# Storing each batch's gates as four rows of 448 bytes, turned on the chip first, in place of 448 elements of 4 bytes

## The chip, the cores and the metric

The kernel runs on one core of one Trainium2 chip. The time is device microseconds (us) of one launch. One launch computes an attention layer, a mixture of experts with one expert per token, and a second dense layer with a normalisation.

## The reference

Four batches of 448 tokens (1792 in all) go through three parts:

```python
scores = scale * (q_n @ k_n^T)            # q, k normalised by their root mean square; 12 heads of 64
x = softmax(scores) @ v                   # (4, 12, 448, 64) -> 1792 x 768

logits = x @ w_gate                       # 1792 x 8
expert_idx = argmax(logits, axis=1)
gate_w = softmax(logits)[token, expert_idx]
out[token] = gate_w * (relu(x @ w1[e]) @ w2[e])      # e: the token's own expert, 768 -> 1024 -> 768

h = out @ w_in; solu = h * softmax(h)     # 768 -> 1024
y = layernorm(solu) * g_ln @ w_out        # 1024 -> 768
```

The change touches the way in which `gate_w`, one number for each token, gets to a table in device memory.

## The kernel before, in words

Attention and routing come first, to about 318 us of the profile. They are not written in program order: each piece of work is a task with an engine, an estimated duration, a priority, what it depends on, and the ring buffers that it takes or uses. The class `Work` (L31) walks through all tasks, at each step takes from those that can start earliest the one of the lowest priority number, and issues its instructions. The order on each engine is therefore the outcome of the whole list: a task that is added, or that asks for a buffer, can move every task that is placed after it. Once issued, each engine executes its instructions strictly in that order, and an instruction that waits holds up all behind it.

Attention works on pairs of heads, six for each batch. For each pair GpSimd (POOL) scales the inputs, TensorE (PE) transposes them (L435), ScalarE (ACT) and VectorE (DVE) split them in a high and a low part (L458, L461), SyncE (SP) starts DMAs that move halves between partitions (L468, tiles `KS`, `QQ`, `K2`, `Q2`), PE multiplies (L497), DVE takes maxima (L508), which are transposed (L520) and copied to `mr` on ACT or DVE (L526, L528), ACT takes exponentials, high and low parts are made (L555, L558), and PE multiplies with the values (L587 to L589, tile `av`). The finished 448 x 128 block `x` goes to the device-memory table `xd` (L721), is transposed (L728) and multiplied with the router's weights (L739).

PSUM buffers for most of PE's short results form one ring `r` of four, named r_99 to r_102 in the instruction lists: a task that takes one waits until all readers of its last holder are done.

After the sixth pair of a batch, `Routing.route` (L761) works out for its 448 tokens, laid out as 112 partitions x 4 columns: the expert (L782 to L840), each token's rank among its expert's tokens (L790 to L797 on PE, L842, L843), four one-hot compares (L809, tile `ohr`), the list of tokens of each expert (L815, 12 short matmuls; L824, L826 or L828), and the gate: exponentials (L855), their sum (L856, L857), its reciprocal `gt` (L832). The gate is stored to the device-memory table `gd`, of one column, with a DMA on SP (L859). `gd` is read much later, by small gathers (L1569).

After the last batch, the lists `gx` are copied to a second table (L984 to L990). GpSimd then gathers the rows of `xd` that belong to each expert (L1129, `gx<-xd,gx`); PE transposes the first expert's rows (L1175) and the experts start (L1154 onwards). Expert weights come by DMA on SP (L1104, `wr`).

Of the kernel before, what the change touches and what calls it, by code (L numbers as in the profile page):

```python
# [7 lines left out]
F32 = mybir.dt.float32  # L8
# [8 lines left out]
CP = 112  # L17
NC = 4
D = 64
S = 448  # L20
# [10 lines left out]
class Work:  # L31
# [11 lines left out]
               DVE=dict(PE=0.2, ACT=0.14, DVE=0.13, Pool=0.16, SP=0.1), Pool=dict(PE=0.2, ACT=0.2, DVE=0.2, Pool=0.0, SP=0.1),  # L43
# [15 lines left out]
    def add(self, eng, dur, fn, deps=(), prio=0.0, take=(), use=(), lat=0.0, dma=0.0):  # L59

        t = len(self.tasks)
        e = eng if isinstance(eng, dict) else {eng: dur}
        self.tasks.append((e, fn, [d for d in deps if d is not None], prio, take, lat, dma))
        for u in list(take) + list(use):
            self.users.setdefault(u, []).append(t)
        return t
# [106 lines left out]
class Attention:  # L173
# [8 lines left out]

    RINGS = dict(
        kq=2, v=2, sq=2, u=2, gsc=3, vj=1, va=3, X=3, op=6, K2=4, mx=2, mr=2, st=2, pf=5, pp=2, r=4, av=2, den=2,
    )

    def __init__(self, nc, ctx, tc, kq, v, ident, groups, work):
# [16 lines left out]
        ps = P("ps", 1, space=PSUM)  # L204
        R = self.RINGS
        for r in ("st", "r", "av"):
# [10 lines left out]
    def start(self, g_qk):  # L217
        nc = self.nc
        R = self.RINGS

# [433 lines left out]
class Routing:  # L654
# [44 lines left out]
        self.gx = C("gx", [128, RT * E_], I32)  # L699
        self.sum = self.acc_d = self.li_d = None  # L700

    RINGS = dict(x=3, xT=2, lg=2, rt=1, gt=2)

    def start(self, w, w_gate, more):

# [55 lines left out]
    def route(self, w, b, prio, M=None, order=None):  # L761

        nc, W = self.nc, self.pool
        V = nc.vector
# [5 lines left out]
        t = {}  # L770
        own = ("rt", b)
        add = lambda eng, dur, fn, deps, take=(), use=(), lat=0.0: w.add(
            eng, dur, fn, deps, prio, take, [own, *use], lat
        )
# [59 lines left out]
        lg, rk, li, gt = ("lg", b), ("r", f"rk{b}"), ("r", f"li{b}"), ("gt", b)  # L834
        d = w.add("DVE", 0.1, room, [self.sum, *self.init_d], prio, take=[own], use=[lg])
        d_s = d = add("DVE", 0.1, lambda e: V.tensor_tensor(t["ls"], self.lg, bc(t["mx"]), op=ALU.subtract), [d], use=[lg])

        d = add("DVE", 0.1, lambda e: V.scalar_tensor_tensor(t["oh"], t["ls"], 0.0, self.desc, op0=ALU.is_ge, op1=ALU.mult), [d])
        d = add("DVE", 0.1, lambda e: V.tensor_reduce(t["cm"], t["oh"], axis=AX.X, op=ALU.max), [d])
        d_o = add("DVE", 0.1, lambda e: V.tensor_tensor(t["o16"], self.desc, bc(t["cm"]), op=ALU.is_equal), [d])  # L840
        d = d_r = add("PE", 0.2, rank, [d_o, self.acc_d], take=[rk])
        d = add("DVE", 0.1, lambda e: V.tensor_tensor(t["rkt"], t["z"].rearrange("p (c e) -> p c e", e=E_), t["o16"], op=ALU.mult), [d], use=[rk])  # L842
        d = add("DVE", 0.1, lambda e: V.tensor_reduce(self.rk[:, bs], t["rkt"], axis=AX.X, op=ALU.add), [d])  # L843
        d_t = add("DVE", 0.1, lambda e: V.tensor_tensor(tk, t["o16"], bc(self.tid[:, bs]), op=ALU.mult), [d_o])
        if M is not None:
# [4 lines left out]
        d = add("PE", 0.28, lists, dd + [d_t], take=[li])  # L850
        d_l = self.li_d = add("DVE", 0.1, total, [d, self.li_d, order], use=[li])
        d = add("DVE", 0.1, lambda e: V.tensor_reduce(t["oc"], t["o16"].rearrange("p c e -> p e c"), axis=AX.X, op=ALU.add), [d_o])
        self.acc_d = add("DVE", 0.1, lambda e: V.tensor_tensor(self.acc, self.acc, t["oc"], op=ALU.add), [d, d_r])

        d = add("ACT", 0.2, lambda e: nc.scalar.activation(t["ls"], t["ls"], AF.Exp), [d_s, d_o])  # L855
        d = add("DVE", 0.1, lambda e: V.tensor_reduce(t["sm"], t["ls"], axis=AX.X, op=ALU.add), [d])  # L856
        d = add("DVE", 0.1, lambda e: V.tensor_scalar(t["sm"], t["sm"], 1e-9, None, op0=ALU.add), [d])  # L857
        d = add("DVE", 0.1, gate, [d], take=[gt])
        add("SP", 0.5, lambda e: nc.sync.dma_start(  # L859
            self.gd[b * S : (b + 1) * S, :].rearrange("(c p) e -> p c e", c=NC), t["gt"]  # L860
        ), [d], use=[gt], lat=1.5)

    def zeros(self):

# [508 lines left out]
def body(tc, kq, v, g_qk, w_gate, wmoe, w_in, w_out, g_ln, out):  # L1373
    nc = tc.nc
    ctx = ExitStack()
    with ctx, tc.manual_schedule():
# [12 lines left out]
        rpool = P(att_ctx, "route", 1)  # L1389
        work = Work({**Attention.RINGS, **Routing.RINGS})  # L1390
        att = Attention(nc, att_ctx, tc, kq, v, ident, GROUPS, work)
# [462 lines left out]
```

## Time and profile before

| | us |
|---|---|
| three runs | 896.51, 899.03, 904.44 |
| median | 899.03 |
| profiled execution, its own time | 896.94 |
| its span, first to last instruction | 895.2 |

Busy time in the span is 811.1 us on PE (91%), 641.4 on DVE (72%), 497.8 on ACT (56%) and 395.1 on POOL (44%). The 16 DMA engines are busy 40.8% of the span for the queue of SP and 4.0% for that of GpSimd. The profile's own time is 2.1 us below the median of the three runs. Attention and routing with the first gathers take the span to 336 us, the experts to about 650 us, the second layer the rest.

### The profile page before, as it was taken

The page shows a single profiled execution, that of the slowest core. Times are in us where ns is not written, and L with a number is a line of the kernel's source. Part 1 is how long each engine was busy: PE and PEld are TensorE (multiplying, and loading weights), DVE is VectorE, ACT ScalarE, POOL GpSimd, SP SyncE. Part 2 cuts the span into 40 slices and gives each one's busy share as a digit, 9 for nine tenths or more (in the row PEclk, how much of TensorE's full clock was granted, in tenths as well). Part 3 has the DMA queues.
Part 4 walks back from the last instruction along what each step waited for, and adds up shares of the span by engine and source line. Part 5 has one row for each costly group of instructions (what it writes and reads, how often), then busy time and mean ns, then how long its engine had stood idle before and what let it go on. Part 6 is the DMA issues. An engine that isn't in the chain of part 4 may idle for free.

```text
span 895.2 us, 18893 instructions
## 1 busy us (share of the span) xinstructions
PE 811.1 (91%) x6811; PEld 740.8 (83%) x6811; DVE 641.4 (72%) x1484; ACT 497.8 (56%) x958; POOL 395.1 (44%) x420
## 2 busy tenths in 40 slices
PE   2788998987898959989999999899899999999994
PEld 2577887776787849979999999789779989998994
DVE  7988998897898937998667778788575434444541
ACT  7787988886885805644455556667532323332221
POOL 4777898787784624543674125545110000000000
PEclk9999999999997979999999999999999999999998
DMA  7476575574743355757666777767000000000001
GB/s 207 125 200 171 134 197 145 146 197 83 198 111 83 117 118 164 222 187 244 209 220 202 260 229 250 243 211 245 2 1 36 19 36 19 18 18 36 19 18 38
DMA packets 63871, 120.29 MB, mean 134 GB/s; under 512 B 12159, under 2 KB 35290, under 8 KB 63774
## 3 DMA queue, kind: packets, MB, share of 16 engines
q1 hardware_dynamic: 60478, 107.69, 40.8%
q0 software_dynamic: 3296, 11.35, 4.0%
q8 instruction: 56, 0.92, 0.4%
q14 instruction: 41, 0.34, 0.1%
HBM read 86.08 MB, written 11.03 MB: 108 GB/s over the span
## 4 chain that ended last, share of the span: by engine, by line
PE 36%; issue 26%; DVE 17%; DMA 13%; ACT 4%; POOL 2%; SPq 1%; POOLq 0%; ACTq 0%; DVEq 0%
DMA out_dram<-ot,tok 5%; PE st L497 4%; DMA QQ<-QQ 3%; PE h L1157 3%; DVE mx L508 2%; PE h L1158 2%; PE y L1157 2%; PE h L1159 2%; PE y L1158 2%; PE y L1159 2%; PE r L497 2%; PE h L1154 2%; DMA gx<-xd,gx 2%; PE y L1154 2%; DMA rkq<-in_kq_dram 2%
## 5 line engine op out<-in xcount | busy, mean ns | idle before, releaser
L558 POOL TENSOR_TENSOR pl<-pf,ph 128x448 f16<-128x448 f32 x153 | 166.1, 1105 | 47.7 <-ACT ph L555 16.8
L1359 POOL DMA_INDIRECT out_dram<-ot,tok x14 | 13.8, 987 | 214.3 <-ACT ot L1358 208.8
L508 DVE TENSOR_REDUCE mx<-r 128x1 f32<-128x448 f32 x168 | 99.4, 611 | 12.3 <-PE r L497 11.9
L1114 POOL TENSOR_TENSOR wl<-wr,wh 128x768 fp32r<-128x768 f32 x34 | 64.5, 1899 | 93.6 <-ACT wh L1109 93.1
L1109 ACT CAST wh<-wr 128x768 fp32r<-128x768 f32 x128 | 104.7, 831 | 1.6 <-DMA wr<-in_wmoe_dram 1.6
L1114 DVE TENSOR_TENSOR wl<-wr,wh 128x768 fp32r<-128x768 f32 x94 | 97.5, 1037 | 10.5 <-ACT wh L1109 9.0
L551 ACT ACTIVATE pf<-st 128x448 f32<-128x448 f32 x168 | 86.7, 544 | 22.0 <-PE st L497 19.5
L497 PE MATMUL r<-KS,QQ 128*128 128x448 f32 x192 | 69.0, 428 | 21.0 <-DMA QQ<-QQ 12.1
L555 ACT CAST ph<-pf 128x448 f16<-128x448 f32 x153 | 82.5, 569 | 0.3
L587 PEld LDWEIGHTS <-ph 128*128 128x128 f16 x768 | 71.0, 97 | 12.0 <-issue 10.9
L587 PE MATMUL av<-va,ph 128*128 128x65 f16 x768 | 80.1, 194 | 0.0
L588 PE MATMUL av<-va,ph 128*128 128x64 f16 x768 | 79.7, 195 | 0.0
L589 PE MATMUL av<-va,pl 128*128 128x65 f16 x768 | 79.3, 193 | 0.0
L497 PE MATMUL st<-QQ,KS 128*128 128x448 f32 x192 | 74.4, 408 | 2.7 <-ACT pf L551 2.6
L1320 DVE TENSOR_TENSOR cl<-ct,ch 128x512 fp32r<-128x512 f32 x28 | 18.1, 686 | 80.3 <-ACT ch L1319 80.2
L589 PEld LDWEIGHTS <-pl 128*128 128x128 f16 x768 | 71.6, 99 | 0.0
L588 PEld LDWEIGHTS <-ph 128*128 128x128 f16 x768 | 71.4, 97 | 0.1
L497 PE MATMUL st<-Q,K 128*128 128x448 f32 x192 | 68.7, 378 | 0.5 <-DMA K<-KS 0.5
L1154 PE MATMUL y<-hh,wh 128*128 128x384 f32 (+1 forms) x192 | 61.0, 354 | 7.7 <-DVE hh L1203 7.4
L1154 PE MATMUL h<-xx,wh 128*128 128x384 f32 (+1 forms) x192 | 63.0, 364 | 0.4 <-DVE xx L1184 0.4
L497 PEld LDWEIGHTS r<-KS,QQ 128*128 128x128 f32 x192 | 35.5, 199 | 31.1 <-DVE mx L508 5.9
L1157 PE MATMUL h<-xx,wh 128*128 128x280 f32 (+1 forms) x192 | 57.4, 299 | 0.7 <-DVE hh L1203 0.7
(282 smaller groups left out, 2525.9 us busy)
## 6 DMA issues: line engine op xcount, KB each, us to landing
wr<-in_wmoe_dram SPq DMA_DIRECT2D x128, 384.0 KB
rkq<-in_kq_dram SPq DMA_DIRECT2D x24, 448.0 KB
di<-in_w_in_dram SPq DMA_DIRECT2D x16, 384.0 KB
rv<-in_v_dram SPq DMA_DIRECT2D x24, 256.0 KB
do<-in_w_out_dram SPq DMA_DIRECT2D x16, 384.0 KB
K<-KS SPq DMA_DIRECT2D x48, 112.0 KB
KS<-Q SPq DMA_DIRECT2D x48, 112.0 KB
QQ<-QQ SPq DMA_DIRECT2D x48, 112.0 KB
```

The source lines that it names most:

```text
L497: nc.tensor.matmul(ps[:, :S], H[w][x + "x"][:, columns(w, s)], H[w][y], start=(k == 0), stop=(k == len(n) - 1))
L508: V.tensor_reduce(C["mx"][:, s : s + 1], C["sm", s][:, :S], axis=AX.X, op=ALU.max, negate=True)
L551: nc.scalar.activation(C["pf", s], C["st", s][:, :S], AF.Exp)
L555: (eng[e].copy if e == "ACT" else eng[e].tensor_copy)(ph[s][:, :S], C["pf", s])
L558: eng[e].tensor_tensor(pl[s][:, :S], C["pf", s], ph[s][:, :S], op=ALU.subtract)
L587: nc.tensor.matmul(o, hp, vs[:, 0:65], start=(s == ss[0]), stop=False)
L588: nc.tensor.matmul(o[:, 0:64], hp, vs[:, 65:129], start=False, stop=False)
L589: nc.tensor.matmul(o, lp, vs[:, 0:65], start=False, stop=(s == ss[-1]))
L1109: self.nc.scalar.copy(wh, raw)
L1114: (eng or self.nc.vector).tensor_tensor(wl, raw, f32(wh), op=ALU.subtract)
L1154: mm(ps[:, : 2 * n], wh, xx[:, : 2 * n], start=start, stop=False)
L1157: mm(ps[:, :n], wh, xh, start=start, stop=False)
```

## The change

The gates `gt` (112 partitions x 4) are transposed on PE into a buffer of the ring `r`, which gives four rows of 112, copied by DVE to a new tile `gq` (4 partitions x 112, two buffers), and stored from there. The table `gd` gets the same bytes at the same places. The four stores had 448 pieces of 4 bytes each; now they have four pieces of 448 bytes each.

```diff
-    RINGS = dict(x=3, xT=2, lg=2, rt=1, gt=2)
+    RINGS = dict(x=3, xT=2, lg=2, rt=1, gt=2, gq=2)
...
         d = add("DVE", 0.1, gate, [d], take=[gt])
+        gr, gq = ("r", f"gr{b}"), ("gq", b)
+
+
+        def rows(e):
+            t["gr"] = w.buf(*gr)
+            nc.tensor.transpose(t["gr"][:NC, :CP], t["gt"][:, :, 0], self.ident[:CP, :CP])
+
+        def copy_rows(e):
+            t["gq"] = W.tile([NC, CP], F32, tag="gq", name=f"gq{b}", bufs=2)
+            V.tensor_copy(t["gq"], t["gr"][:NC, :CP])
+
+        d = add("PE", 0.11, rows, [d], take=[gr], use=[gt])
+        d = add("DVE", 0.12, copy_rows, [d], take=[gq], use=[gr])
         add("SP", 0.5, lambda e: nc.sync.dma_start(
-            self.gd[b * S : (b + 1) * S, :].rearrange("(c p) e -> p c e", c=NC), t["gt"]
-        ), [d], use=[gt], lat=1.5)
+            self.gd[b * S : (b + 1) * S, :].rearrange("(c p) e -> c (p e)", c=NC), t["gq"]
+        ), [d], use=[gq], lat=1.5)
```

Eight instructions are new: four transposes on PE (L864) and four copies on DVE (L868). The store is L872 afterwards, and lines behind it have moved by 13. Up to the routing of the first batch the order is the same as before; from there on every engine's order differs. By count, six copies of maxima to `mr` change from ACT to DVE (18 and 6 before, 12 and 12 after) and so does one making of a high part (153 on ACT before, 152 after).

On SP, around the store of the second batch (`KS`, `K`, `QQ`, `Q` are the moves between partitions; K is `K2` and Q is `Q2`), before:

```order
L468 DMA KS_130<-Q_142 64x448
L859 DMA gd<-gt_3651 112x4x1
L721 DMA xd<-x_1_3483 112x4x128
L468 DMA K_145<-KS_129 64x448
L468 DMA QQ_136<-QQ_136 64x448
L468 DMA KS_125<-QQ_131 64x448
L468 DMA K_146<-KS_130 64x448
L531 DMA Q_139<-mr_115 1x4x128
L531 DMA Q_140<-mr_115 1x4x128
L468 DMA KS_125<-Q_137 64x448
```

and after:

```order
L721 DMA xd<-x_1_3482 112x4x128
L468 DMA QQ_135<-QQ_135 64x448
L872 DMA gd<-gq_3677 4x112
L468 DMA KS_130<-QQ_136 64x448
L468 DMA K_145<-KS_129 64x448
L468 DMA KS_130<-Q_142 64x448
L468 DMA KS_125<-QQ_131 64x448
```

The store of the block `xd` stood right behind that of the gates and now stands two places ahead of it.

On DVE, in the routing of the third batch, before (`ohr` are the one-hot compares, `sm` the sum of exponentials, r_99 to r_102 the ring `r`):

```order
L809 TENSOR_SCALAR ohr_3_4815<-cols,rk 112x384
L857 TENSOR_SCALAR sm_4588<-sm_4588 112x4
L461 SCALAR_TENSOR_TENSOR Q_142<-r_102,G,QQ_136 128x448
L603 TENSOR_SCALAR den_4848<-av_103,ve_3930 112x4
L832 RECIPROCAL gt_4851<-sm_4588 112x4
L508 TENSOR_REDUCE mx_113<-r_99 128x1
```

and after:

```order
L809 TENSOR_SCALAR ohr_3_4833<-cols,rk 112x384
L857 TENSOR_SCALAR sm_4606<-sm_4606 112x4
L508 TENSOR_REDUCE mx_113<-r_100 128x1
L603 TENSOR_SCALAR den_4865<-av_103,ve_3911 112x4
L832 RECIPROCAL gt_4867<-sm_4606 112x4
L508 TENSOR_REDUCE mx_113<-r_102 128x1
L614 RECIPROCAL den_4865<-den_4865 112x4
L826 TENSOR_TENSOR lists<-lists,r_100 128x24
L508 TENSOR_REDUCE mx_113<-r_99 128x1
L608 TENSOR_TENSOR x_1_4894<-av_103,den_4865 112x4x64
L868 COPY gq_4901<-r_102 4x112
```

and on PE at the same place, after:

```order
L815 LDWEIGHTS ohr_3_4833
L815 MATMUL r_100<-tk,ohr_3_4833 128x8
L497 MATMUL st_97<-QQ_131,KS_125 128x448
L497 MATMUL st_97<-Q_137,K_145 128x448
L864 MATMUL r_102<-ident,gt_4867 4x112
L497 MATMUL st_98<-QQ_131,KS_125 128x448
L497 MATMUL st_98<-Q_137,K_145 128x448
```

Behind the compares DVE had a split that frees r_102; now it has two maxima there, which free r_100 for the list matmuls and r_102 for the new transpose, and the gates in between.

On DVE, in the last batch, after:

```order
L832 RECIPROCAL gt_5644<-sm_5618 112x4
L809 TENSOR_SCALAR ohr_0_5646<-cols,rk 112x384
L809 TENSOR_SCALAR ohr_1_5649<-cols,rk 112x384
L809 TENSOR_SCALAR ohr_2_5651<-cols,rk 112x384
L809 TENSOR_SCALAR ohr_3_5653<-cols,rk 112x384
L868 COPY gq_5655<-r_100 4x112
L828 SCALAR_TENSOR_TENSOR gx<-r_102,lists 128x24
```

The copy is the only new row there; it stands between the last compare and the lists.

## Rows read from the trace of the kernel before

**Rows 1.** Windows by stage: busy us of each engine, granted clock, DMA share, GB/s.

```profile
200.00:300.00 100.00, 89.89 (x1131) 79.22 (x1131) 84.34 (x215) 75.68 (x155) 68.64 (x66) 0.93 0.47 112
...
318.00:336.00 18.00, 8.00 (x54) 6.88 (x53) 4.29 (x25) 0.49 (x3) 4.91 (x5) 0.64 0.51 103
```

**Rows 2.** Instructions on the table gd: duration min/median/max in ns, first and last start.

```profile
L859 SPq DMA_DIRECT2D gd<-gt x4: 330/517/537, 135.8 to 321.6; - x4
```

**Rows 3.** DMA queue of SP, 281 to 281.25 us: packets, MB, share of 16 engines.

```profile
q1 hardware_dynamic: 345, 0.00, 70.5%
```

**Rows 4.** Timeline of SP, second batch's store: start us, us, what.

```profile
210.30 0.54 SPq L859 DMA_DIRECT2D gd<-gt  x1
210.93 0.51 SPq L721 DMA_DIRECT2D xd<-x  x1
...
218.85 0.54 SPq L468 DMA_DIRECT2D KS<-Q  x1
```

**Rows 5.** Waits of SP from 208 to 220 us: total us, times, longest.

```profile
SPq L468 <- DMA gd<-gt: 2.3, 1, 2.3
```

**Rows 6.** Windows of 1 us behind the second batch's store, columns as in rows 1.

```profile
212.00:213.00 1.00, 1.00 (x11) 0.94 (x9) 1.00 (x3) 0.96 (x3) 1.00 (x2) 1.00 0.79 215
...
215.00:216.00 1.00, 1.00 (x15) 0.65 (x11) 0.88 (x3) 1.00 (x3) 1.00 (x2) 1.00 1.67 106
...
217.00:218.00 1.00, 0.00 (x0) 0.00 (x0) 0.22 (x1) 0.42 (x2) 1.00 (x2) 1.00 0.41 47
```

**Rows 7.** DMA queue of SP, 213.25 to 213.5 us, as in rows 3.

```profile
q1 hardware_dynamic: 4, 0.00, 196.9%
```

**Rows 8.** Windows of 1 us behind the first and the third batch's store.

```profile
140.00:141.00 1.00, 1.00 (x9) 0.95 (x8) 1.00 (x3) 0.97 (x3) 1.00 (x2) 1.00 0.49 115
...
287.00:288.00 1.00, 1.00 (x5) 0.87 (x4) 0.00 (x0) 0.65 (x2) 0.34 (x1) 0.50 0.51 148
```

**Rows 9.** Timeline of PE from 218.5 us, with idle time before and what ended it.

```profile
219.43 0.64 PE L497 MATMUL r<-KS,QQ 128*128 128x448 f32 x2 [3.39 <-DMA Q<-mr]
```

**Rows 10.** Window of 1 us behind that wait.

```profile
221.00:222.00 1.00, 1.00 (x6) 0.87 (x6) 0.75 (x2) 0.00 (x0) 0.00 (x0) 0.50 0.28 67
```

**Rows 11.** Timeline of POOL: the first expert's first gather.

```profile
324.08 1.19 POOL L1129 DMA_INDIRECT gx<-xd,gx  x1 [10.18 <-DVE pl_gf L984]
```

**Rows 12.** Timeline of PE from 326 us: transposes of the gathered rows.

```profile
332.77 1.51 PE L1175 MATMUL yx<-ident,gx 128*128 128x128 f32 x6 [5.82 <-DMA gx<-xd,gx]
335.22 0.90 PE L1175 MATMUL yx<-ident,gx 64*128 64x64 f32 x6 [0.94 <-DMA gx<-xd,gx]
```

**Rows 13.** DMA queue of GpSimd, 326 to 328 us, then 420 to 422 us.

```profile
q0 software_dynamic: 13, 0.08, 86.2%
...
q0 software_dynamic: 103, 0.53, 83.3%
```

**Rows 14.** Window of the experts' first us, columns as in rows 1.

```profile
335.00:340.00 5.00, 4.39 (x19) 4.21 (x20) 1.68 (x6) 1.43 (x6) 0.48 (x1) 0.50 0.15 48
```

**Rows 15.** Timelines of DVE and PE, last batch's routing.

```profile
323.00 0.18 DVE L828 SCALAR_TENSOR_TENSOR gx<-r,lists 128x24 int32<-128x24 f32 x1 [0.50 <-PE r L873]
...
321.87 1.09 PE L815 MATMUL r<-tkr,ohr 112*128 112x8 f16 x12 [1.27 <-DVE ohr L809]
```

**Rows 16.** Timelines of DVE and PE, third batch's routing, and the window behind it.

```profile
274.71 3.06 DVE L809 TENSOR_SCALAR ohr<-cols,rk 112x384 f16<-112x384 f16 x3
...
279.33 1.01 PE L728 MATMUL r<-ident,x 112*128 112x112 f32 x4 [2.53 <-DVE Q L461]
...
278.50:289.00 10.50, 9.67 (x63) 8.45 (x63) 7.39 (x20) 4.71 (x9) 3.53 (x5) 0.51 0.20 45
```

**Rows 17.** Groups by line and shape, 100 to 325 us: busy, mean ns of one.

```profile
L520 PE MATMUL r<-ident,mx 128*7 128x128 f32 x17 | 4.6, 272 | 0.0
...
L528 DVE TENSOR_SCALAR mr<-r 7x128 fp32r<-7x128 f32 x4 | 1.1, 273 | 1.2 <-PE r L520 1.2
...
L555 DVE CAST ph<-pf 128x448 f16<-128x448 f32 x11 | 5.7, 516 | 0.0
```

## The prediction, made before the result was known

> **What bounds the kernel now.** I read the windows by stage first. Up to 318 us no engine is the bound by itself: PE, DVE, ACT and POOL wait for each other in short turns, with PE and DVE the fullest (89.89 and 84.34 us of 100 from 200 to 300 us) [rows 1]. Between 318 and 336 us nearly everything stands: PE is busy 8.00 of 18 us, at a mean granted clock of 0.64 [rows 1]. There the last batch's routing, the lists and the first gather follow one another, and each us is a us of the launch. From 336 us the experts keep PE busy, so an earlier start of the experts carries to the end, and a later one too.
>
> The four stores of gates that change are small in every view: SP spends 517 ns on the issue of one [rows 2], and in the fullest quarter of a us 345 of the 4-byte packets take 70.5% of 16 engines [rows 3], which is 0.705 x 0.25 x 16 / 345 = 8 ns each, so about 0.25 us for 448 of them if 16 engines share them. By that the change would be worth nothing. So I looked at what happens behind each store.
>
> Behind the second batch's store something does. It is issued at 210.30 us, and the store of `xd` right behind it [rows 4]. The next us of packets is normal (215 GB/s at 0.79 of the engines). Then the DMA engines are full and move little: 106 GB/s at a share of 1.67, then 47 GB/s at 0.41 [rows 6], and in one quarter of a us four packets take 196.9% of 16 engines, 2.0 us each [rows 7]. SP stands 2.3 us for the landing of the gate store and goes on at 218.85 us [rows 5, 4], 8.55 us after its issue. [...] I call this the wake of the store.
>
> The last batch's store, at 321.6 us [rows 2], is followed by the stores of the table `tab` and then by the first expert's gather, issued at 324.08 us [rows 11]. From 326 to 328 us GpSimd's queue moves 13 packets with 86.2% of 16 engines: 0.862 x 2 x 16 / 13 = 2.1 us each. In a later gather it is 103 packets with 83.3%, 0.26 us each [rows 13]. The 2.1 us is the same as in the second batch. PE waits 5.82 and 0.94 us for the two gathers and begins the second at 335.22 us [rows 12].
>
> Against a common cause speak the first and the third store. Some us behind them, at 140 and 287 us, 115 and 148 GB/s move at shares of 0.49 and 0.51, as in any quiet stretch [rows 8]. What differs is the next write: behind the second store comes `xd`, behind the fourth `tab`, behind the first and third no further write to device memory for some us. My theory is that 448 writes of 4 bytes land slowly, over some 7 us, and that another write to device memory behind them, within that time, fills the engines.
>
> **The change part by part.** *The last batch's gather.* A later gather moves 0.53 MB in 2 us [rows 13]. The first two gathers are 192 rows of 3 KB, 0.59 MB, 2.2 us at that pace, and one load of weights beside them (128 x 768 numbers, 0.39 MB) another 1.5 us. The first issue ends at 325.27 us (324.08 + 1.19) [rows 11], so both could have landed at 329.0, where PE begins at 335.22: 6.2 us. The second gather is issued later than the first and the third and fourth share the engines, so I take 5.0, between 0 (the wake is not the store's) and 6.2. Next late then is the gathers' own transfer. A shorter stop could also keep PE's clock up: from 335 to 340 us it is 0.50 [rows 14], which would give 2.5 us more; I take none of it.
>
> *The second batch's wait.* The stop of 3.39 us [rows 9] and some 3 us at half clock behind it (1.6 us lost) give at most 5.0. The moves would need some time to land in any case, and the new order puts `xd` ahead of the store. I take 1.5, between 0 and 5.0.
>
> [...]
>
> *What is added.* Four transposes on PE, by the nearest row (a transpose to 7 x 128) 0.27 us each, and four copies on DVE, by the copy of 7 x 128 out of PSUM 0.27 us each [rows 17]. In the last batch both are hidden: PE idles 1.27 us ahead of the list matmuls, and the gates are ready ahead of the compares; the copy stands in the 0.50 us in which DVE waits for PE ahead of `gx` [rows 15]. Without that cover it would be 0.3 us on the path. The store itself comes some 1 us later on SP, ahead of the stores of `tab`, which wait for a later instruction of DVE. In the other three batches DVE is nearly full: 3 x 0.27 = 0.8 us, between 0 and 1.6 (PE's part too).
>
> *What is moved.* Everything behind the first batch's store (135.8 us) [rows 2] is placed anew. By count DVE gets six copies of maxima (0.27) and one cast (0.52) from ACT [rows 17]: 2.2 us more on an engine that is one of the two fullest. I take half, 1.1, between 0 and 2.2.
>
> *The new waits.* PE's transpose waits for the gates and for its buffer, and all of PE's later work is queued behind it. In the first two batches the order leaves PE enough ahead of it. In the third, the list matmuls and then the transpose wait for DVE, which makes the compares (three take 3.06 us), a maximum, the gates and a second maximum first. The old order stops PE at the same place: 2.53 us for a split behind the compares, and 9.67 us of work at a clock of 0.51 behind it [rows 16], which costs about 9.67 x 0.49 = 4.7. A stop for a stop, I take 0, between -7.2 (it is gone, with its slow clock) and +7.2 (a second one like it).
>
> Sum: -5.0 - 1.5 + 0.8 + 1.1 + 0 = -4.6 us. The profiled execution took 896.94 us, so 892.3; its own time is 2.1 below the median of 899.03, so the median of new runs may lie up to 2 us higher. I predict 892.
>
> **The rivals.** *The wake is not the store's, or stays.* The slow packets at 326 us are the first of GpSimd's queue, and two of the four stores show no wake. Then the first two terms are 0: 896.94 + 1.9 = 898.8 us.
>
> *PE waits at the new transpose.* It ends on the other side. In the third batch L864 stands two matmuls behind the lists, and needs a gate and a buffer that DVE gives four places behind its last compare. If PE empties there, and the clock falls, each such stop costs up to 7.2 us. It decides from a stop of about 2 us, since the old one was 2.53. With one stop and no gain at the gather: 898.8 + 7.2 = 906.0; with a second one in the second batch 913.
>
> *More than the sum.* PE's stop in the third batch goes (-7.2), and the experts begin at full clock (-2.5): 892.3 - 9.7 = 882.6 us. For it speaks that both stops follow from DVE's or the gather's lateness alone; against it that the new DVE order has as many rows behind its compares.
>
> **How the numbers follow.** I give the forecast 0.50, no wake 0.22, the new wait 0.12, more than the sum 0.16. A range from 883 to 903 leaves out about half of the last case and most of the third, 0.19 in all. The three runs before lie 7.9 us apart, so 1% (9.0 us, 890.0 to 908.0) is about what a measurement can tell from no change. Faster by more: the last case and 0.10 of the forecast, 0.26. Slower by more: 0.07, of the third case. The rest, 0.67, is within 1%.
>
> **What would show it.** Right: the first packets of GpSimd's queue at about 0.3 us each, PE's transposes of the second gather some 6 us behind the first gather's issue, where they are 11.1 us behind now, no stretch in attention with a share over 0.9 and under 110 GB/s, SP never standing for a gate store. Wrong: the same 2 us packets behind the new stores; a wait of PE at L864 of over 1 us, or the end of attention moved by more than 5 us, by an order that no row here prices. The last is the likeliest way to be wrong, in either direction.

## The result, and the profile after

The changed kernel takes 888.68 us (median of six runs, 882.16 to 892.86) where the kernel before took 899.18 in the runs beside it: a ratio of 0.9869 with a 95% interval of 0.9823 to 0.9915. Six more runs gave 890.52 us and 0.9849 (0.9806 to 0.9892). So it is faster by 1.3 to 1.5%. The profiled execution took 887.74 us, its span is 886.0, 9.2 us less than before.

The first gather, on POOL's and PE's timelines of the changed kernel (start us, us, engine, line, what; in brackets the idle time before and what ended it):

```profile
318.12 1.19 POOL L1142 DMA_INDIRECT gx<-xd,gx  x1 [11.06 <-DMA gd<-gq]
...
323.16 1.51 PE L1188 MATMUL yx<-ident,gx 128*128 128x128 f32 x6 [1.87 <-DMA gx<-xd,gx]
324.83 0.90 PE L1188 MATMUL yx<-ident,gx 64*128 64x64 f32 x6 [0.16 <-DMA gx<-xd,gx]
```

From the issue to the transposes of the second gather it is 6.71 us, where it was 11.14 [rows 11, 12]. The issue itself comes 5.96 us earlier, so 4.4 us were gained in the gather and 6.0 ahead of it. (The bracket names the landing of the new store as what released the gather, but the issue comes 5.18 us behind L782 of the last batch in both kernels, so this costs nothing.) Some 1.2 us of the 10.4 are given back among the experts.

GpSimd's queue from 320 to 322 us, behind the new store (packets, MB, share of 16 engines):

```profile
q0 software_dynamic: 66, 0.37, 69.4%
```

That is 0.694 x 2 x 16 / 66 = 0.34 us for a packet, where it was 2.1 [rows 13].

Windows of the changed kernel, columns as in [rows 1]: the third batch's routing, a stretch in the second batch, the experts' first us:

```profile
278.50:289.00 10.50, 10.50 (x141) 9.34 (x140) 10.00 (x25) 8.43 (x17) 6.79 (x6) 1.00 0.35 89
199.00:210.00 11.00, 10.54 (x93) 9.71 (x93) 6.99 (x23) 7.13 (x16) 5.21 (x5) 0.54 0.46 130
...
325.00:330.00 5.00, 4.61 (x21) 4.43 (x22) 1.68 (x6) 1.71 (x8) 0.88 (x1) 0.54 0.19 70
```

The stretch that ran at a clock of 0.51 behind the third batch's stop [rows 16] is at 1.00 and PE is never idle in it. There is a new slow stretch at 199 us in this execution; in that of e11, the same kernel, the same window has a clock of 0.95. The experts begin at a clock of 0.54, where it was 0.50 [rows 14].

The new instructions on PE and DVE: duration min/median/max in ns, first and last start:

```profile
L864 PE MATMUL r<-ident,gt x4: 259/260/346, 138.8 to 315.7; 112*4 112x112 f32 x4
...
L868 DVE COPY gq<-r x4: 252/252/255, 139.7 to 316.5; 4x112 f32<-4x112 f32 x4
```

### The profile page after: what moved, and what is told of

The parts are those of the page before. It is cut to its first block, busy times and chain, and to the rows that moved or that the text cites. A ratio compares the mean times of both kernels' runs of the same rounds, so it can differ in the third digit from the quotient of the medians.

```text
span 886.0 us, 18898 instructions
## 1 busy us (share of the span) xinstructions
PE 810.0 (91%) x6815; PEld 739.9 (84%) x6815; DVE 641.6 (72%) x1495; ACT 497.9 (56%) x951; POOL 397.3 (45%) x420
## 4 chain that ended last, share of the span: by engine, by line
PE 38%; issue 26%; DVE 14%; DMA 13%; ACT 4%; POOL 2%; SPq 1%; another core or an unknown queue 1%; POOLq 0%; ACTq 0%; DVEq 0%
DMA out_dram<-ot,tok 5%; PE st L497 5%; PE r L497 3%; PE h L1170 3%; DMA QQ<-QQ 2%; PE h L1171 2%; PE h L1167 2%; PE h L1172 2%; PE y L1170 2%; DMA KS<-QQ 2%; PE y L1171 2%; PE y L1172 2%; DMA rkq<-in_kq_dram 2%; DVE mx L508 2%; PE y L1167 2%
## 5 line engine op out<-in xcount | busy, mean ns | idle before, releaser
L1127 DVE TENSOR_TENSOR wl<-wr,wh 128x768 fp32r<-128x768 f32 x94 | 97.0, 1032 | 11.1 <-ACT wh L1122 9.4
L587 PEld LDWEIGHTS <-ph 128*128 128x128 f16 x768 | 71.4, 98 | 12.4 <-issue 11.1
L497 PE MATMUL r<-KS,QQ 128*128 128x448 f32 x192 | 66.0, 415 | 14.0 <-DMA QQ<-QQ 9.3
L588 PEld LDWEIGHTS <-ph 128*128 128x128 f16 x768 | 71.8, 98 | 0.2
L423 POOL TENSOR_TENSOR X<-rkq,y 128x512 f32<-128x512 f32 (+1 forms) x48 | 47.7, 1006 | 19.0 <-DVE y L347 16.0
```

What stands on the lines that cost most here:

```text
L497: nc.tensor.matmul(ps[:, :S], H[w][x + "x"][:, columns(w, s)], H[w][y], start=(k == 0), stop=(k == len(n) - 1))
L587: nc.tensor.matmul(o, hp, vs[:, 0:65], start=(s == ss[0]), stop=False)
L588: nc.tensor.matmul(o[:, 0:64], hp, vs[:, 65:129], start=False, stop=False)
L1127: (eng or self.nc.vector).tensor_tensor(wl, raw, f32(wh), op=ALU.subtract)
```

## The experiments

All kernels are listed here, because the stages tell more than the totals. The three stages are the times between the starts of the routing's first maximum (L782) of batches 1 to 4 on DVE, each from one profiled execution; "gather" is the time from the issue of the first gather to PE's second six transposes. Each ratio is to runs of the kernel before on the same chip, so compare kernels by the ratios and not by the times. In the kernel before, for example, L782 starts at 118.58, 191.65, 265.90 and 318.90 us.

| kernel | order | store | us | ratio to before, 95% | 1-2 | 2-3 | 3-4 | gather |
|---|---|---|---|---|---|---|---|---|
| before | old | 448 x 4 B | 899.18 | | 73.1 | 74.3 | 53.0 | 11.1 |
| e1 | new | 448 x 4 B | 903.53 | 1.0015 (0.9987-1.0044) | 76.1 | 70.2 | 57.0 | 11.9 |
| e4 | old | 448 x 4 B, write behind | 904.51 | 1.0024 (0.999-1.0058) | 78.0 | 74.7 | 51.7 | 11.5 |
| e6 | old | 448 x 4 B, ACT's queue | 903.35 | 1.0016 (0.9985-1.0047) | 76.0 | 79.7 | 49.0 | 12.1 |
| e2 | old | 4 x 448 B | 892.57 | 0.9915 (0.9886-0.9943) | 72.3 | 75.2 | 52.3 | 6.5 |
| e3 | old | 112 x 16 B | 888.39 | 0.9834 (0.978-0.9887) | 72.1 | 71.8 | 53.0 | 6.8 |
| e10 | old | 448 x 16 B | 894.66 | 0.9905 (0.987-0.9941) | 73.3 | 71.1 | 53.0 | 6.6 |
| e7 | old | one of 16 x 448 B | 892.64 | 0.9886 (0.9845-0.9928) | 73.7 | 72.7 | 51.8 | 6.3 |
| changed | new | 4 x 448 B | 888.68 | 0.9869 (0.9823-0.9915) | 72.6 | 71.5 | 49.5 | 6.7 |
| e11, the same | new | 4 x 448 B | 890.52 | 0.9849 (0.9806-0.9892) | 71.4 | 70.9 | 49.8 | 6.9 |
| e8 | new | one of 16 x 448 B | 885.66 | 0.9849 (0.9802-0.9897) | 72.5 | 68.7 | 49.0 | 7.8 |
| e12, as e8 | new | one of 16 x 448 B | 890.80 | 0.9846 (0.9806-0.9885) | 72.0 | 70.4 | 49.0 | 7.0 |

In e2 PE makes all twelve transposes without a stop, the first of them 4.93 us behind the issue.

**e1, the new order with the old form.**

```diff
-            self.gd[b * S : (b + 1) * S, :].rearrange("(c p) e -> c (p e)", c=NC), t["gq"]
-        ), [d], use=[gq], lat=1.5)
+            self.gd[b * S : (b + 1) * S, :].rearrange("(c p) e -> p c e", c=NC), t["gt"]
+        ), [d], use=[gq, gt], lat=1.5)
```

> The changed kernel with its order, transposes and copies, but each store again writes 448 pieces of 4 bytes from the untransposed gates, at the place where the changed kernel stores the rows. Theory of the wake (small pieces, and a write to device memory behind them): in this order no such write follows the second batch's store closely, but the table's store follows the fourth, so the second batch stays without a stop and the first gather is slow again, some 11 us from its issue to PE's transposes of the second gather (6.7 in the changed kernel): 4.4 us over the changed kernel, 893 us, ratio to before 0.993. Rival, the order alone makes the gain: as the changed kernel, 888.7 us, 0.988, gather at 6.7 us. Rival, any store of this form slows what comes behind it: stops behind two or more of the stores, 897 us or more.

It measured 903.53 us, a ratio of 1.0015 whose interval holds 1: the last rival, and not the 0.993 that I expected. The gather is slow, and SP stands behind the first and the third store, where I had seen no wake. SP's waits in the 10 us behind the third store of e1 (total us, times, longest), and the move in question on its timeline:

```profile
SPq L468 <- DMA KS<-QQ: 4.3, 1, 4.3
```

```profile
283.15 0.46 SPq L468 DMA_DIRECT2D KS<-QQ  x1
...
289.45 0.46 SPq L468 DMA_DIRECT2D QQ<-QQ  x1
```

The same place in the changed kernel, whose order is the same:

```profile
SPq L468 <- DMA KS<-QQ: 0.2, 1, 0.2
```

```profile
279.33 0.46 SPq L468 DMA_DIRECT2D KS<-QQ  x1
...
281.51 0.46 SPq L468 DMA_DIRECT2D QQ<-QQ  x1
```

`QQ<-QQ` overwrites what `KS<-QQ` reads, so it waits for the landing of that move: 2.18 us behind its issue in the changed kernel, 6.30 us in e1. The windows of e1 show nothing of it, since the engines are nearly or wholly idle meanwhile:

```profile
287.00:288.00 1.00, 1.00 (x29) 1.00 (x29) 1.00 (x4) 0.86 (x2) 0.97 (x2) 1.00 0.16 16
288.00:289.00 1.00, 1.00 (x28) 0.99 (x26) 0.86 (x1) 0.07 (x1) 1.00 (x2) 1.00 0.00 0
```

The kernel before has the same thing in its first batch, where I had looked at windows only [rows 8]. SP's waits in the 10 us behind its first store:

```profile
SPq L468 <- DMA KS<-QQ: 2.2, 1, 2.2
```

and PE behind them:

```profile
147.00 0.64 PE L497 MATMUL r<-KS,QQ 128*128 128x448 f32 x2 [2.17 <-DMA QQ<-QQ]
```

In all four kernels with 448 x 4 bytes PE has such a stop behind the first store, of 2.16 to 2.83 us; in the eight others no stop of PE for a move in stage 1-2 is over 1.5 us.

**e2, the new form in the old order.**

```diff
...
-            V.reciprocal(t["gt"], t["sm"])
+            V.reciprocal(t["gt"], t["sm"].to_broadcast([CP, NC, 28]))
...
-            self.gd[b * S : (b + 1) * S, :].rearrange("(c p) e -> p c e", c=NC), t["gt"]
+            self.gd[b * S : (b + 1) * S, :].rearrange("(c p) e -> c (p e)", c=NC),
+            t["gt"][:NC].rearrange("p c e -> p (c e)")
```

> The kernel before, with its order and without transposes, but each store writes four pieces of 448 bytes. What is left out: the rows hold the gates of four partitions, repeated, and not each token's own, so the output is scaled by wrong gates. Theory of the wake: no packets of 2 us behind any store, the gather at 6 to 7 us (4.4 gained), no wait of SP for the gate store in the second batch (1.5 to 5 gained), the stop in the third batch stays: 890 to 893 us, ratio 0.990 to 0.993. Rival, the order alone makes the gain: 899 us, ratio 1.000, with the wake or the stops as before. Rival, all of the gain is the form's: 888.7 or less, 0.988.

It measured 892.57 us, 0.9915: as the theory of the wake has it. SP waits for no landing in the 10 us behind any of the first three stores. The third batch's stop stays as it was:

```profile
281.25 0.60 PE L728 MATMUL r<-ident,x 112*128 112x112 f32 x4 [2.53 <-DVE Q L461]
```

**e3, 112 pieces of 16 bytes in the old order.**

```diff
-            self.gd[b * S : (b + 1) * S, :].rearrange("(c p) e -> p c e", c=NC), t["gt"]
+            self.gd[b * S : (b + 1) * S, :].rearrange("(p c) e -> p (c e)", c=NC), t["gt"][:, :, 0]
```

> The kernel before, with its order, but each store writes 112 pieces of 16 bytes (the four gates of a partition side by side). What is changed: the gates stand at other tokens' places in the table. If the wake counts by pieces: a quarter of its length, about 2 us behind the second and the fourth store in place of 7, the time within 1 us of the kernel with four pieces of 448 bytes. If any store of small pieces has it: as before, 899 us, packets of 2 us for some 7 us. If order makes the gain and not the store: 899 us too, but without a change of the gather.

It measured 888.39 us, 0.9834, without a late move and with a gather of 6.8 us. A quarter of the pieces, at 16 bytes, leaves nothing of the wake where I had expected a quarter of its length. That pieces of this size make it is out.

**e4, a write behind the first and third store.**

```diff
...
+            if b in (0, 2):
+                nc.sync.dma_start(
+                    self.sd[b * S : (b + 1) * S, :].rearrange("(c p) e -> p c e", c=NC),
+                    self.zero[:CP, :512].rearrange("p (c e) -> p c e", c=NC),
+                )
```

> The kernel before with one more store of 112 x 4 x 128 zeros to an unused table, right behind the gate stores of the first and the third batch, where none follows before. Theory of the wake: a second and a third wake there, full DMA engines with packets of about 2 us for some 5 us around 140 and 285 us, and late moves between partitions: 901 to 909 us, ratio 1.002 to 1.011. Rival, the wake belongs to the second batch's and the gather's own neighbours: no full engines there, only two issues of 0.5 us on SP and 1.3 us of transfers, 899 to 900 us.

It measured 904.51 us; the interval of the ratio holds 1. Behind the third store the engines are full for 1 us (a window of e4), behind the first SP takes 3.58 us over the issue of one move (its timeline):

```profile
290.00:291.00 1.00, 1.00 (x7) 1.00 (x7) 1.00 (x2) 0.55 (x1) 0.64 (x1) 0.50 1.38 133
```

```profile
144.23 3.58 SPq L468 DMA_DIRECT2D K<-KS  x1
```

So the time doesn't decide, and the trace shows the theory half right at most. A write behind isn't needed for a late landing (e1). It may lengthen it: in the first batch SP issues the `QQ<-QQ` that waits for the move 9.9 us behind the store, against 7.5 us before, but PE's stop there is 2.23 us against 2.17.

**e6, the old store on ACT's queue.**

```diff
-        add("SP", 0.5, lambda e: nc.sync.dma_start(
+        add("SP", 0.5, lambda e: nc.scalar.dma_start(
```

> The kernel before with its order and its form of store, issued from ACT's queue at the same place of the program and not from SP's. Theory that landings are held up in the order of one queue: SP no longer waits for moves behind the first three stores, about 4 of the 7.7 us that the form alone gains are seen, the gather stays slow (its cause is the write, not SP's queue): 895 to 897 us, ratio 0.995 to 0.997. Rival, the 4-byte writes hold up the engines or the memory for all queues: late moves as before, 899 us or more, ratio 1.00 to 1.005.

It measured 903.35 us, 1.0016, the rival. SP waits 2.4 us for a move in the first batch and 3.3 us for the landing of the store in the second. The order within one queue is not what holds the moves.

**e5 and e9, trials behind the work.** Each trial issues a store, a move of 64 x 448, and a small transfer that waits for the move.

```diff
...
+            if k != "m":
+                dma(dst(s), src)
+            dma(mv[64:128], a[0:64, :448])
+            dma(dv[0:1, :4], mv[64:65, :4])
```

> The kernel before, and behind all of its work twelve trials on SP's queue, with no other transfers: a store of one form (or none), a move of 64 x 448 between partitions right behind it, a small transfer that waits for the move, and a second store to the same table that waits for the first. SP's issue times give the landings. Theory (a store of many 4-byte pieces lands late, and what is queued behind it lands no sooner): the move alone 2 to 2.5 us; behind 448 pieces of 4 bytes 5 to 8 us, as the store itself; behind 4 pieces of 448, 112 of 16 or 448 of 512 bytes as alone, within 1 us. Of the dose: 112 pieces of 4 bytes a quarter of the delay, 224 a half, if pieces count. With 448 pieces of 4 bytes spread at 512 bytes apart: the same delay if the count of small pieces makes it, none if neighbouring pieces in one 512-byte stretch do. Rival (the delay needs the other traffic of attention): no trial lands the move later than 3 us.

> A second row of trials of the same kind behind the work: the move alone (2.2 us in the first row of trials), then behind 16, 28 and 112 pieces of 4 bytes side by side; 112 pieces of 4 bytes at 8, 16 and 64 bytes from one to the next; 112 and 448 pieces of 8 bytes, 448 of 16, 448 of 64, side by side; last, 448 pieces of 4 bytes with the move on ACT's queue. Theory (pieces that fall in one small stretch of memory wait for each other): the delay falls as fewer pieces share a stretch, 112 pieces at 64 bytes near 2.2 us, at 8 and 16 bytes between 2.2 and 6; 112 pieces of 8 bytes about 4, 448 of 16 at 2.2 to 3, 448 of 64 at 2.2. If the stretch is some 512 bytes: at 64 bytes still over 3 us. Since 112 pieces of 4 bytes took 6.04 and 448 took 7.1 us, 16 and 28 pieces: near 6 if it is a fixed price, 1 us or less over the move alone if it is by pieces. Theory that the queue is not what holds the move: on ACT's queue 6 to 8 us too; rival, the queue's order: 2.2.

SP's timeline in e5: the move alone (L1747, then L1748 when it has landed), then a store of 448 x 4 bytes (L1743) with its move:

```profile
886.15 0.55 SPq L1747 DMA_DIRECT2D pm<-pa  x1
888.44 0.68 SPq L1748 DMA_DIRECT2D pd<-pm  x1
889.24 0.35 SPq L1743 DMA_DIRECT2D ps<-pa  x1
890.14 0.53 SPq L1747 DMA_DIRECT2D pm<-pa  x1
897.38 0.63 SPq L1748 DMA_DIRECT2D pd<-pm  x1
```

So a move lands after 888.44 - 886.15 = 2.29 us alone and after 7.24 behind the store. Read in this way, all trials:

| store ahead of the move | landing of the move, us |
|---|---|
| none, twice in e5, once in e9 | 2.29, 2.17, 2.26 |
| 448 x 4 B side by side, twice | 7.24, 6.98 |
| 224 x 4 B, 112 x 4 B, 28 x 4 B side by side | 6.29, 6.04 (e9: 6.11), 2.35 |
| 448 x 4 B, 512 bytes apart | 2.21 |
| 112 x 4 B, 8, 16, 64 bytes apart | 2.60, 2.19, 2.22 |
| 112 x 8 B, 448 x 8 B side by side | 2.81, 3.55 |
| 112 x 16 B, 448 x 16 B, 448 x 64 B | 2.20, 2.22, 2.18 |
| 4 x 448 B, 448 x 512 B | 2.21, 2.63 |
| 448 x 4 B and 448 x 512 B | 8.18 |
| 4 x 448 B and 448 x 512 B | 2.55 |
| 448 x 4 B, the move on ACT's queue | 7.06 |

16 x 4 B took 4.30 us, but 80 packets of GpSimd's queue and two of instructions moved in that trial, and I leave it out. The first 448 x 4 B had as much beside it; its repeat (6.98) and the trials of 224 and 112 had no packets of GpSimd's queue. So the delay needs no other traffic. It isn't the count (448 pieces 512 bytes apart: 2.21 us) nor small pieces as such (16 bytes: 2.20 and 2.22): it takes many 4-byte pieces side by side (6.04 to 7.24 behind 112 to 448), and 8-byte pieces side by side show a small part of it (2.81 and 3.55). Most forms were tried once. The dose that I had expected by count failed: 112 pieces take nearly what 448 take (6.04 us against 7.24 and 6.98), and 28 next to nothing (2.35). The windows of e5's last trial (move issued at 961.39, landed at 968.37 us) show the engines done by 964:

```profile
962.00:963.00 1.00, 0.00 (x0) 0.00 (x0) 0.00 (x0) 0.00 (x0) 0.00 (x0) 0.50 0.37 88
963.00:964.00 1.00, 0.00 (x0) 0.00 (x0) 0.00 (x0) 0.00 (x0) 0.00 (x0) 0.50 0.12 27
964.00:965.00 1.00, 0.00 (x0) 0.00 (x0) 0.00 (x0) 0.00 (x0) 0.00 (x0) 0.50 0.00 0
```

**e10, the same 448 pieces at 16 bytes, in the old order.**

```diff
...
-        gd = dpool.tile([NT + 1, 1], F32, name="gd")
+        gd = dpool.tile([NT + 1, 4], F32, name="gd")
...
+            V.reciprocal(t["gt"], t["sm"].to_broadcast([CP, NC, 4]))
...
```

> The kernel before with its order and its 448 pieces, but the table has rows of four numbers and each gate is written four times, so a piece is 16 bytes; the small gathers read every fourth number, with one more multiplication of their indices on DVE in the experts' part. Theory (many 4-byte pieces crowded in one stretch of memory land late; the same count at 16 bytes landed a move at 2.2 us): no late moves, gather at 6 to 7 us, as four rows in the old order, 890 to 894 us, ratio 0.988 to 0.993. Rival, the count of pieces in real traffic matters after all: 897 to 900 us, gather over 9 us.

It measured 894.66 us, 0.9905, with a gather of 6.6 us. The trials hold in the kernel itself: the late moves and the slow gather go with the crowded 4-byte writes, not with the number of pieces, and they go without any transposes.

**e7 and e8, one store of all gates behind the last batch, in the old and the new order.**

```diff
...
+            V.reciprocal(self.gall[:, bs].unsqueeze(2), t["sm"])
...
+        nc.tensor.transpose(gr, rt.gall, ident[:CP, :CP])
+        nc.vector.tensor_copy(gq, gr)
+        nc.sync.dma_start(gd[0:NT, :].rearrange("(a p) e -> a (p e)", p=CP), gq)
```

> The kernel before with its order, but no store of gates in attention: the gates of all batches stay in one tile, and behind the lists of the last batch one transpose, one copy and one store of 16 rows of 448 bytes write them all. If the form is the whole gain and order is neutral: no late moves, the gather at 6 to 7 us, as the four-row stores in the old order, 891 to 893 us, ratio 0.990 to 0.9925, less up to 1 us for three stores fewer. If the new order is what makes the changed kernel faster than that: it stays 3 to 4 us behind the changed kernel.

> The same one store of 16 rows in the order of the changed kernel; the four transposes, four copies and four stores in attention are gone, their places in the order are kept empty. If the added instructions cost what I took (0.8 us): 888, ratio 0.986 to 0.988. If they are hidden: as the changed kernel, 888.7, 0.987. If the transposes' waits matter (PE stops at them in the first and the last batch for 1.1 us each): 886 to 887, 0.985.

> The changed kernel itself once more, beside the next kernel on the same chip: 886 to 890 us, ratio 0.983 to 0.9915 as in its first runs.

> The one store of 16 rows in the order of the changed kernel once more, beside it. If the transposes and copies that it saves cost what I took (0.8 us): 0.5 to 1.5 us under the changed kernel, not told apart by their intervals. If its first runs (885.66, 0.9849 against 0.9869) show more than that: 2 to 3 us under it.

e7 is 892.64 us (0.9886), as the four-row stores in the old order. e8 began at 885.66 us, but in the second pair of runs, on one chip, it took 890.80 and the changed kernel 890.52 us (just over the 886 to 890 that I expected): the same, within 4 us to either side by their intervals. What the added transposes, copies and stores cost is not told by that; 0.8 us would not show.

**What the order does.** In all seven kernels of the old order PE stops at L728 (L729 in e7) in the routing of the third batch for 2.52 or 2.53 us, in the five of the new order not at all. DVE's three compares there take 3.05 to 3.07 us in all seven, and 0.95 or 0.96 us in the five. Third batch, DVE's and POOL's timelines, changed kernel (before: 3.06 us [rows 16]):

```profile
275.04 0.96 DVE L809 TENSOR_SCALAR ohr<-cols,rk 112x384 f16<-112x384 f16 x3
275.92 0.16 DVE L857 TENSOR_SCALAR sm<-sm 112x4 f32<-112x4 f32 x1
...
271.78 3.65 POOL L558 TENSOR_TENSOR pl<-pf,ph 128x448 f16<-128x448 f32 x3 [0.78 <-PE r L728]
275.94 1.03 POOL L558 TENSOR_TENSOR pl<-pf,ph 128x448 f16<-128x448 f32 x1 [0.52 <-ACT ph L555]
```

and before:

```profile
277.69 0.99 DVE L857 TENSOR_SCALAR sm<-sm 112x4 f32<-112x4 f32 x1
...
274.60 5.05 POOL L558 TENSOR_TENSOR pl<-pf,ph 128x448 f16<-128x448 f32 x5 [0.62 <-PE r L435]
```

Before, the compares and L857 lie beside five subtractions of POOL without a gap; in the changed kernel POOL pauses there. Over all twelve kernels there are 192 such compares: each of the 71 that take 0.50 us or more has a subtraction of POOL beside it for over three quarters of its time, and the 86 with no work of POOL beside them take at most 0.32 us. The other 35 have POOL beside them for a part and are as fast (0.31 us at 130.25 us before), so POOL is not enough by itself. That POOL slows the compares is my guess from these rows; no run here moved POOL's work alone, so it is not shown. Nor does a run part the speed of the compares from the rows around them: the new order has also put a split (L461) ahead of the three compares, where the old one has behind them the split that PE waits for.

What the stop costs seems to come by the clock. Stage 3-4 in before, in e6, which has the same stop (2.52 us), and in the changed kernel, which has none:

```profile
265.90:318.90 53.00, 48.90 (x737) 43.84 (x735) 43.82 (x112) 35.13 (x72) 28.67 (x26) 0.90 0.38 106
```

```profile
279.88:328.92 49.04, 44.91 (x737) 40.26 (x735) 42.85 (x112) 34.98 (x72) 28.94 (x26) 1.00 0.43 116
```

```profile
263.41:312.94 49.53, 46.43 (x745) 41.04 (x743) 42.62 (x115) 36.10 (x73) 29.82 (x27) 1.00 0.46 126
```

The same 737 matmuls keep PE busy 4.0 us longer in before than in e6, and the stage is 4.0 us longer. In six of the seven kernels of the old order the clock of the stage is 0.90 to 0.93; e6, at 1.00, is as short as the new order. So the stop came with a fall of the clock in six executions and without one in the seventh.

## Why the prediction was right and where it was not

892 was predicted, 888.7 and 890.5 came, inside the range, faster by a little over 1%, the case I gave 0.26; 0.67 lay within 1%. The number is nearer than the sum deserves. The sum gained 4.6 us; between the two profiled executions 9.2 were gained: 4.4 in the gather, 6.7 in stages 1 to 4, less 0.7 ahead of them and 1.2 among the experts. That 892 is close is partly luck: I began at the profiled execution, 2.1 us below the median. All four signs of being right came, and two of being wrong: a wait of over 1 us at L864, and an end of attention moved by more than 5 us (the gather's issue by 5.96).

**The gather (-5.0): right in cause, 4.4 measured.** The four kernels with 448 x 4 bytes need 11.1 to 12.1 us, the eight others 6.3 to 7.8. The experts' first us ran at a clock of 0.54 where it was 0.50 [rows 14]; I had taken no gain from it.

**The second batch's wait (-1.5): gone, its worth not told; and the theory behind it failed at "against a common cause speak the first and the third store".** PE's stop of 3.39 us (3.63 in e4, 4.59 in e6) is in none of the eight kernels with another store, nor in e1, where the new order alone has it gone. In the four with another store in the old order stage 2-3 takes 72.7 us on the mean against 74.3, but 71.1 to 75.2 singly, and PE's next stop, 2.32 us at 238 us before, takes 2.85 to 4.11 us in them; the new order has neither. I read the wake from packets, and packets are not landings. Behind the first and third stores too moves landed late (2.2 us of SP's wait and 2.17 of PE's behind the first store before, 4.3 us of SP's in e1's third batch), with engines that were not full (0.49 [rows 8], 0.16 and 0.00 in the windows of e1). A write behind the store is not the condition; what is needed is somebody who waits. One queue's order is not it either: in the trials the move lands 7.06 us after its issue on ACT's queue, and 7.24 and 6.98 on SP's. What holds the landing up was not shown. Nor does a row ahead of the prediction show that stores of 448-byte pieces leave no wake, on which the gains of the sum rested; the trials show it for pieces of 448 bytes (2.21 us) as for pieces of 16 (2.20 and 2.22).

**What is added (+0.8) and moved (+1.1): not told.** The instructions took 0.26 and 0.25 us where I took 0.27. e12, which has one transpose and one copy in place of four each, is no faster than e11 beside it, but their intervals are 4 us wide to either side, and its stages 1 to 4 are 0.9 us shorter in single executions. So 0.8 is neither borne out nor refuted. The moved copies of maxima were not measured apart from the rest of the order.

**The new waits (0, from -7.2 to 7.2): the step that failed.** "A stop for a stop" was wrong: I took the 3.06 us of the compares over into the new order, where they take 0.96, so PE's stop and its slow clock are gone in that batch, and the stage 3-4 fell from 53.0 to 49.5 us, 3.5 of the 7.2 that I had as the bound. I had added the stop to its slow clock; in e6, with the stop and without the slow clock, the stage takes 49.0. PE does wait at L864 in the last batch:

```profile
315.70 0.35 PE L864 MATMUL r<-ident,gt 112*4 112x112 f32 x1 [1.06 <-DVE gt L832]
```

That stop takes the place of the 1.27 us ahead of the list matmuls [rows 15], which then follow at once; none of the first three batches has a stop there (what I expected of e8 names one in the first, which is not in the rows).

**Form and order may not be a sum.** Stages 1 to 4 together take 200.3 us before; 203.3 with the new order alone (e1); 198.1 with another form alone (mean of e2, e3, e7, e10); 191.8 with both (mean of changed, e11, e8, e12). With the gather's 4.4 the sum for both is 12.9 us; the ratios say 11.8 to 13.9 (0.9869 to 0.9846 of 900). For the form alone it is 6.6, and the ratios say 7.6 to 14.9 (e2, e10, e7, e3). So with the old store the new order gains nothing that the runs show (e1's interval holds 1), and with another store it gains 6.3 us by the stages. The runs don't show that gain: e3, in the old order, has the lowest ratio of all, 0.9834, and the intervals of single kernels of the two orders overlap. The stage times are of single executions, which scatter by some us between kernels of one kind (2-3 most, 68.7 to 75.2). That the order gains rests on the stage 3-4, its stop and its clock: 49.0 to 49.8 us in the new order but for e1, whose late move stops PE there for 2.36 us, and 51.7 to 53.0 in the old but for e6.

Open: why a move behind 112 neighbouring 4-byte writes lands only after 6.04 to 6.11 us, and one behind 28 of them after 2.35; whether POOL is what slowed the compares; why the clock did not fall behind e6's stop (1.00 in its stage 3-4); and how much of the gain is the order's.

## What to carry to other kernels

Don't store a column of 112 or more 4-byte numbers piece by piece where something soon after waits for a DMA: here a move behind 112 to 448 of them landed after 6.04 to 7.24 us, and after 2.17 to 2.29 alone. What left it at that pace was to give each piece 16 bytes (2.20 and 2.22), to spread 112 of them 16 bytes apart (2.19), or to gather them into rows of 448 bytes (2.21). Look for the cost in what waits for the landing of transfers behind the store (time from a move's issue to the instruction that it releases, beside the same move elsewhere), not in packets or engine shares. And when a planner re-orders everything, keep the old form once in the new order and the new form once in the old, and compare stops and clock stage by stage, since the totals of a few runs may not tell the two apart.

## What was not expected of the hardware

In the last trial of e5 the engines are idle from 964 us, 3.5 us behind the issue of 448 writes of 4 bytes at 960.47, and the move behind them has landed only at 968.37, 7.9 us behind it; a move on another queue was as late (7.06 us). For 112 such writes, 8 bytes from piece to piece in place of 4 takes a delay of 3.85 us (6.11 against 2.26) to 0.34 (2.60), and 16 bytes leave none (2.19).
